# One Trainium2 core: weight decoding of the first gated layer moved into PSUM banks and off GpSimd, with later output sums and freer engine choice

## The chip, the cores and the metric

The kernel runs on one core of one Trainium2 chip. The metric is the device time of one launch in microseconds (us): lower is better. The median of three runs before the change is 941.42 us (940.76 to 943.93). PE is TensorE (matrix products), DVE is VectorE, ACT is ScalarE, POOL is GpSimd, and SP is SyncE, whose queue here issues all the transfers.

## The reference

The program computes three layers in a row, all in float32 at the interface:

```python
# 1 attention with a running state: B=4, H=8, S=768, D=48
for t in range(S):
    cur = einsum('bhd,bhe->bhde', u[None] * kt, vt)
    y[:, :, t] = einsum('bhd,bhde->bhe', rt, state + cur)
    state = wt[:, :, :, None] * state + einsum('bhd,bhe->bhde', kt, vt)
x = y.transpose(0, 2, 1, 3).reshape(3072, 384)
# 2 gated layer, d_ff = 1536
x = (1 / (1 + exp(-(x @ w_gate))) * (x @ w_val)) @ w_out
# 3 second layer, d_ff = 2048
h = x @ w_in
return (h * tanh(softplus(h))) @ w_out2
```

Matrix products of full precision are made of float16 pieces: each operand is split into a high and a low float16 part, and three products of parts are added up.

## The kernel before

The sequence is cut into 24 steps of 32 positions, j, and 12 pairs of steps, p. For a pair, POOL and DVE build the decayed inner products of the positions in `fine` (tiles blk, pt, A), DVE transposes r, k and w into RD, KD, WD and KT, PE forms the coarse scores lp, and eight small copies shared by ACT and DVE ("merges", `merge`, L664) put them into X. Then `step` runs on PE: yp (the outputs of 32 positions), xp (their transposition) and kp (the update of the state s). The copies of KT into KK ("gathers", `gather`, L705) come before kp, and yp becomes xs and then xt, the input of the gated layer for 256 rows.

The gated layer of pair p is six gates, i = 0 to 5 (`gate`). A gate has two blocks of 128 columns for the gate (weights wgs, tile gv with last digit 0) and two for the value (wvs, last digit 1). One block is nine matmuls of 128x256, called a product below. ACT takes the sigmoid, DVE multiplies (L905), ACT writes the high half of gt (L917) and DVE the rest (L920). `out1` adds the gated values times wos into three sums per pair (o10_0 is pair 0, sum 0), each in four parts of nine matmuls, in the PSUM tile of the bank po. The gates use the PSUM banks pg0 to pg3 in turn: three of them in pair 0, all four afterwards.

The weights of the gated layer arrive as float64 words. Eighteen chunks of 128x768 (six each of wg, wv, wo) are loaded into three raw tiles in turn, and each is decoded: ACT makes the low bits ("low", L239) and a rebased word (L249), DVE joins them, ACT casts the high float16 half, and a fourth instruction subtracts to get the low half (called the rest below). Before the change the even chunks (all wg) are decoded by `decode_early` in halves of 128x384, one in the PSUM bank pg3 and one in po, with the rest on DVE (L401). The odd chunks (all wv) and all of wo are decoded whole in SBUF by `decode`, with the rest on DVE or POOL (L307).

The order of the work is a plan: every `add` or `attn` call gives a task, its engine or a choice of engines with costs, and the keys it reads and writes. `Plan.run` places the tasks by due time on each engine, and the instructions are issued in that order. Engines run their own queue strictly in order and wait for each other through semaphores, so what stands behind a waiting instruction waits too.

Of the kernel before, what the change touches and what calls it, by code (L numbers as in the profile page):

```python
# [25 lines left out]
DM = H * D  # L26
# [134 lines left out]
def mixer_moe_kernel(  # L161
# [199 lines left out]
    def decode_early(name, i, dst, src, count):  # L361

        slot = count % 3
        raw = ("raw", slot)
        low = ("low", count % 2)
        key = (name, i)
        load_raw(key, lambda: dp, src, (KC, 256), slot)

        def bits3(e):
            lows[key] = dp.tile([128, KC, 256], U32, tag=f"low{count % 2}", name=f"low_{name}{i}")  # L370
            spare_bits(key)

        add("act", 1.1, bits3, [raw, "consts"], [low])
        for h in range(2):
            f = 2 * i + h
            hs = slice(128 * h, 128 * h + 128)
            fs = slice(128 * f, 128 * f + 128)
            bank = (("pg", 3), "po")[h]

            def rebase(e, h=h, hs=hs, f=f):  # L380
                pool, tag = ((pg, "pg3"), (po, "po"))[h]
                t = pool.tile([128, 512], F32, tag=tag, name=f"word_{name}{f}")
                words[name, f] = t[:, : KC * 128].rearrange("p (a b) -> p a b", a=KC)
                rebased(words[name, f], raws[key][:, :, hs, 1])

            def join(e, hs=hs, f=f):
                bits = words[name, f].bitcast(U32)
                nc.vector.scalar_tensor_tensor(
                    out=bits,
                    in0=bits,  # L390
                    scalar=3,
                    in1=lows[key][:, :, hs],
                    op0=ALU.logical_shift_left,
                    op1=ALU.bitwise_or,
                )

            def high(e, fs=fs, f=f):
                nc.scalar.copy(out=dst[:, 0, :, fs], in_=words[name, f])

            def rest(e, fs=fs, f=f):  # L400
                nc.vector.tensor_tensor(  # L401
                    out=dst[:, 1, :, fs],
                    in0=words.pop((name, f)),
                    in1=dst[:, 0, :, fs],
                    op=ALU.subtract,
                )
# [82 lines left out]
    def fine(p):  # L489
# [27 lines left out]

# [65 lines left out]
    def coarse(p, cells):  # L583
# [25 lines left out]
        def flip_w(e):  # L609

            wd[p] = w = ap.tile([128, 7, BH], F32, tag=f"WD{p % 2}", name=f"WD{p}")
            nc.vector.transpose(out=w[:, :4], in_=window(C * (DH + DP), 8 * DH, 4))
            for n, o in ((4, 4), (6, 6)):
                k = n // 2 if n == 4 else 1
                i = 0 if n == 4 else 4
                nc.vector.tensor_tensor(  # L616
                    out=w[:, o : o + k],
                    in0=w[:, i : i + 2 * k : 2],
                    in1=w[:, i + 1 : i + 2 * k : 2],
                    op=ALU.mult,  # L620
                )
# [46 lines left out]
        attn("dve", 1.05, lambda e: flip_r(e, 1), [R], [(*RD, 2)])  # L668
# [12 lines left out]
    def keys(p):  # L681
# [16 lines left out]
                in_=rows(p)[1].rearrange("p t d -> p d t"),  # L698
            )

        def gather(g, q, h):
# [3 lines left out]
            nc.scalar.copy(out=whole, in_=own)  # L705

        attn("pool", 1.0, lambda e: update(e, 8), [W], [K])
        attn("pool", 0.2, join, [], [W])
# [237 lines left out]
    def out1(p, c, part):  # L946
# [17 lines left out]

        reads = [("gt", p % 2, f // 2, a) for f in fr for a in range(2)]
        reads.append(("gt", p % 2, "tile"))
        reads += [("wo", f // 2, a) for f in fr for a in range(2)]
# [352 lines left out]
    for p in range(NP):  # L1320
        for f in range(NF1):
# [103 lines left out]
```

## Time and profile before

| what | value |
|---|---|
| median of three runs | 941.42 us |
| the profiled execution, its own time | 939.37 us |
| its span, first to last instruction | 937.7 us |
| busy: PE, DVE, ACT, POOL | 93%, 71%, 51%, 52% |
| mean granted clock of PE | 0.991 |

The shares are means over stages. In the page's forty slices (23.4 us each) PE is at 0, 4, 7, 8 and 7 tenths in the first five and at 9 from the sixth on, while DVE is at 7 to 9 and POOL at 8 to 9 tenths in the first five. All of the first layer's weights, the first three pairs of attention and the first twelve gates lie in the first 140 us.

### The profile page before, as it was taken

The page shows a single profiled execution, that of the slowest core. Times are in us where ns is not written, and L with a number is a line of the kernel's source. Part 1 is how long each engine was busy: PE and PEld are TensorE (multiplying, and loading weights), DVE is VectorE, ACT ScalarE, POOL GpSimd, SP SyncE. Part 2 cuts the span into 40 slices and gives each one's busy share as a digit, 9 for nine tenths or more (in the row PEclk, how much of TensorE's full clock was granted, in tenths as well). Part 3 has the DMA queues.
Part 4 walks back from the last instruction along what each step waited for, and adds up shares of the span by engine and source line. Part 5 has one row for each costly group of instructions (what it writes and reads, how often), then busy time and mean ns, then how long its engine had stood idle before and what let it go on. Part 6 is the DMA issues. An engine that isn't in the chain of part 4 may idle for free.

```text
span 937.7 us, 29380 instructions
## 1 busy us (share of the span) xinstructions
PE 874.2 (93%) x12808; PEld 703.9 (75%) x12808; DVE 661.3 (71%) x1094; ACT 479.1 (51%) x1065; POOL 487.7 (52%) x528
## 2 busy tenths in 40 slices
PE   0478799999999999999999999999999999999998
PEld 0366678888888888888888886667677676776788
DVE  7999985766785868677688888775655556555541
ACT  2769855352525333342528667675555655556540
POOL 8999931726565464637472275553433434334330
PEclk9989899999999999999999999999999999999999
DMA  9457742213223322232114930010200102000000
GB/s 314 135 166 227 239 119 73 60 47 81 74 60 84 83 56 72 65 85 59 53 47 119 261 102 13 12 40 2 68 1 18 52 1 69 1 19 18 1 34 35
DMA packets 56464, 71.89 MB, mean 77 GB/s; under 512 B 20752, under 2 KB 37648, under 8 KB 56208
## 3 DMA queue, kind: packets, MB, share of 16 engines
q1 hardware_dynamic: 56336, 70.03, 25.3%
q8 instruction: 100, 1.64, 0.8%
q14 instruction: 28, 0.23, 0.1%
HBM read 56.64 MB, written 9.44 MB: 70 GB/s over the span
## 4 chain that ended last, share of the span: by engine, by line
PE 78%; DVE 11%; ACT 5%; DMA 3%; issue 2%; POOL 1%; SPq 0%; ACTq 0%; DVEq 0%; POOLq 0%
PE gv L889 22%; PE h L1067 20%; PE o L1182 18%; PE o L957 13%; PE yp L737 2%; PE kp L829 2%; DVE X L664 1%; ACT X L664 1%; PE lp L643 1%; DMA raw_wp<-wo 1%; ACT KK L705 1%; DVE A L507 1%; DVE KD L605 1%; DVE WD L616 1%; DVE pt L487 1%
## 5 line engine op out<-in xcount | busy, mean ns | idle before, releaser
L1067 PE MATMUL h<-x,wis 128*128 128x512 f16 x864 | 199.9, 379 | 0.0
L889 PE MATMUL gv<-xt,wgs 128*128 128x256 f16 x1296 | 168.8, 277 | 10.5 <-DVE gt L920 7.3
L957 PE MATMUL o<-gt,wos 128*128 128x256 f16 x1296 | 166.9, 274 | 6.4 <-DVE wos L307 2.7
L889 PE MATMUL gv<-xt,wvs 128*128 128x256 f16 x1296 | 166.3, 274 | 1.3 <-DVE gt L920 0.7
L1101 POOL TENSOR_TENSOR sum<-e 128x256 f32<-128x256 f32 x96 | 71.4, 744 | 183.1 <-ACT e L1078 182.9
L487 POOL TENSOR_TENSOR blk<-blk 128x384 f32<-128x384 f32 (+3 forms) x139 | 123.6, 904 | 53.2 <-DMA blk<-rkw 33.7
L889 PEld LDWEIGHTS <-wgs 128*128 128x128 f16 x1296 | 126.5, 99 | 28.9 <-ACT X L664 6.0
L1067 PEld LDWEIGHTS <-wis 128*128 128x128 f16 x864 | 83.5, 98 | 82.9
L957 PEld LDWEIGHTS <-wos 128*128 128x128 f16 x1296 | 125.7, 98 | 25.8 <-DVE wos L307 3.4
L889 PEld LDWEIGHTS <-wvs 128*128 128x128 f16 x1296 | 126.4, 98 | 18.0 <-POOL wvs L307 1.1
L487 POOL TENSOR_TENSOR pt<-blk 128x384 f32<-128x384 f32 x93 | 107.0, 1175 | 50.3 <-DMA blk<-rkw 48.8
L1078 ACT ACTIVATE e<-h 128x512 f32<-128x512 f32 x96 | 57.3, 597 | 84.1 <-PE h L1067 83.2
L900 ACT ACTIVATE sig<-gv 128x512 f32<-128x512 f32 x72 | 43.0, 600 | 86.3 <-PE gv L889 86.0
L917 ACT CAST gt<-gv 128x512 f16<-128x512 f32 x72 | 42.0, 584 | 72.8 <-DVE gv L905 72.6
L1182 PE MATMUL o<-wps,gt 128*128 128x192 f16 x612 | 74.0, 246 | 0.0
L905 DVE SCALAR_TENSOR_TENSOR gv<-gv,sig 128x512 f32<-128x512 f32 x72 | 50.4, 702 | 25.6 <-PE gv L889 20.3
L624 POOL TENSOR_TENSOR RD<-RD,WD 128x256 f32<-128x256 f32 (+2 forms) x32 | 33.6, 1050 | 63.2 <-PE lp L643 32.9
L1120 DVE SCALAR_TENSOR_TENSOR gt<-e,gt 128x256 f16<-128x256 f32 x41 | 27.5, 682 | 49.7 <-ACT gt L1115 49.7
L920 DVE TENSOR_TENSOR gt<-gv,gt 128x512 f16<-128x512 f32 x72 | 49.3, 684 | 16.6 <-ACT gt L917 15.6
L1182 PE MATMUL o<-wps,wgs 128*128 128x192 f16 x498 | 59.4, 246 | 0.0
L664 ACT COPY X<-lp 24x64 f32<-24x64 f32 x159 | 40.7, 256 | 34.1 <-DVE X L664 25.9
L1182 PE MATMUL o<-wps,wos 128*128 128x192 f16 x456 | 57.1, 246 | 0.0
(109 smaller groups left out, 1490.4 us busy)
## 6 DMA issues: line engine op xcount, KB each, us to landing
v<-vt SPq DMA_DIRECT2D x96, 96.0 KB, 2.6
blk<-rkw SPq DMA_DIRECT2D x22, 384.0 KB, 3.8
raw_wi<-wi SPq DMA_DIRECT2D x8, 768.0 KB, 5.1
raw_wp<-wo SPq DMA_DIRECT2D x8, 768.0 KB, 5.8
blk<-rkw SPq DMA_DIRECT2D x11, 512.0 KB, 3.9
raw_wg<-wg SPq DMA_DIRECT2D x6, 768.0 KB, 6.2
raw_wv<-wv SPq DMA_DIRECT2D x6, 768.0 KB, 6.5
raw_wo<-wo SPq DMA_DIRECT2D x6, 768.0 KB, 5.4
```

Of the source, the lines that this page charges most:

```text
L487: engines[e].tensor_tensor(out=pv, in0=a, in1=b, op=ALU.mult)
L664: put(out=xp[p][o : o + t, xs, t:], in_=lps[p, e][i : i + t, :, c : c + C - t])
L889: nc.tensor.matmul(gps[p, i, o][:, h], w[:, a, kc, fs], xt[p][:, c, kc, :], start=(n == 0), stop=(n == 3 * KC - 1),)
L900: nc.scalar.activation(out=sgs[p, i], in_=gps[p, i, 0], func=AF.Sigmoid, scale=1.0 / (SW * SX))
L905: nc.vector.scalar_tensor_tensor(out=gps[p, i, 1], in0=gps[p, i, 1], scalar=SG / (SW * SX), in1=sgs.pop((p, i)), op0=ALU.mult, op1=ALU.mult,)
L917: nc.scalar.copy(out=gt[p][:, 0, 2 * i : 2 * i + 2], in_=gps[p, i, 1])
L920: nc.vector.tensor_tensor(out=gt[p][:, 1, 2 * i : 2 * i + 2], in0=gps[p, i, 1], in1=gt[p][:, 0, 2 * i : 2 * i + 2], op=ALU.subtract,)
L957: nc.tensor.matmul(ops[p, c][:, :NT], wos[:, a, f, cs], gt[p][:, g, f, :], start=(f == 0 and n == 0), stop=(f == NF1 - 1 and n == 2),)
L1067: nc.tensor.matmul(hps[r, f], w2["wi"][:, a, kc, fs], x2[r][:, c, kc, :], start=(n == 0), stop=(n == 3 * KC - 1),)
L1078: nc.scalar.activation(out=es[r, f], in_=hps[r, f], func=AF.Mish, scale=ih)
L1101: engines[e].tensor_tensor(out=sums[0][:, n - 1], in0=a(), in1=b(), op=op)
L1182: nc.tensor.matmul(ops2[h, first], home(slots[r, i, name])[:, c, tsl], w2["wp"][:, a, w, i, :], start=(new and n == 0), stop=(n == 3 * NF2 ...
```

## The change

Four edits, all of them in how the first 140 us are planned, though the last reaches all pairs.

- All eighteen chunks go through `decode_early`: halves of 128x384, the even block in bank pg3, the odd one in po, the rest always on DVE. POOL has no decoding left in this layer. A half of wo is one block f, so wos is now written block by block.
- The gates keep to three banks until gate 8 (6p+i up to `FREE`), because pg3 is in use for longer.
- The parts of pair 0's output sums are issued by the table `FIRST`, from f = 2 of pair 1 on, where one part per f stood before.
- The planner may put gathers on ACT or DVE, the product with U on DVE or POOL, and the two joining products of WD on DVE or POOL.

```diff
-WHOLE = range(1, 12, 2)
+FIRST = ((), (), (0,), (1,), (2,), (3,), (4,), (5,), (6, 7), (8,), (9,), (10, 11))
+FREE = 8
...
-            bank = (("pg", 3), "po")[h]
...
+            w = [(name, i if name == "wo" else f, a) for a in range(2)]
+            w = [(*x, h) if name == "wo" else x for x in w]
             add("act", 0.43, rebase, [raw, "table1"], [bank])
             add("dve", 0.48, join, [low], [bank])
-            add("act", 0.39, high, [bank], [(name, f, 0)])
-            add("dve", 0.47, rest, [bank, (name, f, 0)], [(name, f, 1)])
+            add("act", 0.39, high, [bank], [w[0]])
+            add("dve", 0.47, rest, [bank, w[0]], [w[1]])
...
-                attn("dve", 1.2, times_u, ["U"], [pt])
+                attn({"dve": 1.2, "pool": 1.9}, 0, times_u, ["U"], [pt])
...
-        attn("dve", 1.3, flip_w, [W], [WD])
+        attn("dve", 0.32, flip_w, [W], [WD])
+        attn({"dve": 1.3, "pool": 0.7}, 0, joined_w, [], [WD])
...
-                        "act", 0.51, lambda e, a=(g, q, h): gather(*a), ["KT"], [("KK", p % 2, g, q, h)]
+                        {"act": 0.51, "dve": 0.47},
...
-        n = 4 if p else 3
+        n = 4 if 6 * p + i > FREE else 3
...
-            if p > 0:
+            if p == 1:
+                for n in FIRST[f]:
+                    out1(0, n // 4, n % 4)
+            elif p:
...
-            if count in WHOLE:
-                load_raw((name, i), lambda: dp, in_cols(w, cs), (KC, 256), count % 3)
-                part = lambda dst=dst, cs=cs: dst[:, :, :, cs]
-                both = [2 * i, 2 * i + 1]
-                decode((name, i), part, (KC, 256), count, count % 3, (), W1HI, W1LO, False, both)
-            else:
-                decode_early(name, i, dst, in_cols(w, cs), count)
+            decode_early(name, i, dst, in_cols(w, cs), (KC, 256), count, halves)
...
-        decode(("wo", i), dst, (2, DM), i, i % 3, (), W1HI, W1LO)
+        decode_early("wo", i, wos, in_rows(wo1, cs), (2, DM), count, halves)
```

Where the planner moves the queues shows at three places.

POOL, before pair 0's first scores. lp0 on PE waits for the first two products of RD0 with WD0. Before:

```order
L487 TENSOR_TENSOR pt_161<-blk1_135 128x768
L624 TENSOR_TENSOR RD0_158<-RD0_158,WD0_165 128x32x8
L487 TENSOR_TENSOR pt_175<-blk1_135 128x384
L624 TENSOR_TENSOR RD0_158<-RD0_158,WD0_165 128x32x16
L487 TENSOR_TENSOR blk1_135<-blk1_135 128x16x24
```

and after:

```order
L486 TENSOR_TENSOR pt_148<-blk1_119 128x768
L486 TENSOR_TENSOR pt_154<-blk1_119 128x384
L486 TENSOR_TENSOR blk0_95<-blk0_95 128x4x24
L486 TENSOR_TENSOR blk1_119<-blk1_119 128x16x24 x2
L486 TENSOR_TENSOR blk0_95<-blk0_95 128x2x8x24
L486 TENSOR_TENSOR pt_181<-blk1_119 128x8x48 x2
L626 TENSOR_TENSOR RD0_156<-RD0_156,WD0_175 128x32x8
L486 TENSOR_TENSOR blk0_95<-blk0_95 128x24
L626 TENSOR_TENSOR RD0_156<-RD0_156,WD0_175 128x32x16
```

Work on blk1 (pair 1) that followed RD0 now precedes it.

DVE, around gate 0 of pair 0, whose last instruction (gt0) frees the bank for the third gate. KT is pair 1's transposed k, X1 its merged scores. Before:

```order
L696 STREAM_TRANSPOSE KT_92<-blk1_135 128x24x32
L905 SCALAR_TENSOR_TENSOR gv0_0_1_605<-gv0_0_1_605,sig_645 128x512
L401 TENSOR_TENSOR wgs_88<-word_wg4_529,wgs_88 128x3x128
L388 SCALAR_TENSOR_TENSOR word_wg5_571<-word_wg5_571,low_wg2_517 128x384
L487 TENSOR_TENSOR pt_569<-pt_569,U_94 128x768
L507 TENSOR_REDUCE A_91<-pt_592 128x16
L507 TENSOR_REDUCE A_91<-pt_569 128x32
L507 TENSOR_REDUCE A_91<-pt_663 128x8x2x2
L920 TENSOR_TENSOR gt0_784<-gv0_0_1_605,gt0_784 128x512
L624 TENSOR_TENSOR RD1_509<-RD1_509,WD1_576 128x32x24
L664 COPY X1_620<-lp1_0_717 24x8x8
```

and after, in two pieces, the first up to the first merge, the second from the last merge on:

```order
L913 SCALAR_TENSOR_TENSOR gv0_0_1_605<-gv0_0_1_605,sig_647 128x512
L389 SCALAR_TENSOR_TENSOR word_wg4_588<-word_wg4_588,low_wg2_518 128x384
L389 SCALAR_TENSOR_TENSOR word_wg5_617<-word_wg5_617,low_wg2_518 128x384
L699 STREAM_TRANSPOSE KT_92<-blk1_119 128x24x32
L402 TENSOR_TENSOR wgs_88<-word_wg4_588,wgs_88 128x3x128
L709 COPY KK_93<-KT_92 32x16x24 x4
L666 COPY X1_651<-lp1_0_718 24x8x8
```

```order
L666 COPY X1_651<-lp1_1_719 24x8x8
L666 COPY X1_651<-lp1_1_719 16x8x16
L666 COPY X1_651<-lp1_1_719 8x8x24
L928 TENSOR_TENSOR gt0_680<-gv0_0_1_605,gt0_680 128x512
L389 SCALAR_TENSOR_TENSOR word_wv4_887<-word_wv4_887,low_wv2_595 128x384
```

Four gathers have come to DVE, the product with U and three sums have left this place, and gt0 has moved from before the merges to behind them.

DVE after the change, before the first output sum o10_0, which takes the bank po once the last odd half (word_wo11) is done. X2 and KT are pair 2's:

```order
L666 COPY X2_1582<-lp2_0_1512 8x8x24
L389 SCALAR_TENSOR_TENSOR word_wo9_1616<-word_wo9_1616,low_wo4_1497 128x384
L848 TENSOR_TENSOR s4_904<-kp3_1_1181,s4_904 128x384
L699 STREAM_TRANSPOSE KT_92<-blk2_279 128x24x32
L402 TENSOR_TENSOR wos_90<-word_wo9_1616,wos_90 128x384
L913 SCALAR_TENSOR_TENSOR gv1_0_1_1397<-gv1_0_1_1397,sig_1414 128x512
L709 COPY KK_93<-KT_92 32x16x24
L389 SCALAR_TENSOR_TENSOR word_wo11_1715<-word_wo11_1715,low_wo5_1584 128x384
L709 COPY KK_93<-KT_92 32x16x24 x2
L402 TENSOR_TENSOR wos_90<-word_wo11_1715,wos_90 128x384
```

Before the change the wo chunks stood ahead of KT and of X2's merges, and o10_0's first two parts ahead of all of pair 1's gates on PE; now two and a half gates, lp2 and yp4 stand ahead of o10_0.

## Rows read from the trace of the kernel before

**Rows 1.** Stretches: length, busy PE, PEld, DVE, ACT, POOL, granted clock, DMA share, GB/s

```profile
66.00:97.00 31.00, 26.68 (x541) 20.58 (x539) 28.65 (x51) 26.98 (x54) 30.36 (x27) 0.89 0.63 205
97.00:105.00 8.00, 3.17 (x16) 1.76 (x17) 8.00 (x8) 7.24 (x10) 7.84 (x7) 0.69 0.64 204
...
140.00:500.00 360.00, 355.90 (x6870) 314.28 (x6868) 263.01 (x420) 141.00 (x337) 192.06 (x200) 1.00 0.25 66
```

**Rows 2.** Timeline of PE: start, us, instruction, count, idle before

```profile
23.48 1.78 PE L643 MATMUL lp<-RD,KD 64*32 64x48 f32 x128 [23.48 <-POOL blk L487]
...
48.99 2.10 PE L889 MATMUL gv<-xt,wgs 128*128 128x256 f16 x9
...
65.79 2.08 PE L889 MATMUL gv<-xt,wgs 128*128 128x256 f16 x9 [5.90 <-DVE gt L920]
...
76.63 3.53 PE L889 MATMUL gv<-xt,wgs 128*128 128x256 f16 x18
...
96.72 0.27 PE L957 MATMUL o<-gt,wos 128*128 128x256 f16 x1
...
99.81 0.28 PE L957 MATMUL o<-gt,wos 128*128 128x256 f16 x1 [1.94 <-ACT wos L304]
102.61 1.46 PE L957 MATMUL o<-gt,wos 128*128 128x256 f16 x6 [2.52 <-DVE wos L307]
...
105.33 1.88 PE L889 MATMUL gv<-xt,wgs 128*128 128x256 f16 x9
...
133.00 1.16 PE L889 MATMUL gv<-xt,wvs 128*128 128x256 f16 x9
133.99 1.15 PE L957 MATMUL o<-gt,wos 128*128 128x256 f16 x9
```

**Rows 3.** Timeline of POOL, the work on blk1

```profile
22.40 2.03 POOL L487 TENSOR_TENSOR blk<-blk 128x384 f32<-128x384 f32 x2
```

**Rows 4.** DVE, 10 to 125 us by shape: count, busy us, mean ns, idle before

```profile
L293 DVE SCALAR_TENSOR_TENSOR word_wo<-word_wo,low_wo 128x768 uint32<-128x768 uint32 x6 | 8.4, 1421 | 0.0
...
L293 DVE SCALAR_TENSOR_TENSOR word_wv<-word_wv,low_wv 128x768 uint32<-128x768 uint32 x6 | 7.3, 1219 | 0.1
L388 DVE SCALAR_TENSOR_TENSOR word_wg<-word_wg,low_wg 128x384 uint32<-128x384 uint32 x12 | 6.6, 551 | 0.3 <-ACT word_wg L249 0.3
L401 DVE TENSOR_TENSOR wgs<-word_wg,wgs 128x384 f16<-128x384 f32 x12 | 6.5, 544 | 0.0
...
L487 DVE TENSOR_TENSOR pt<-pt,U 128x768 f32<-128x768 f32 x3 | 4.1, 1377 | 0.0
...
L307 DVE TENSOR_TENSOR wos<-word_wo,wos 128x768 f16<-128x768 f32 x2 | 3.4, 1751 | 0.0
```

**Rows 5.** POOL, the same stretch by shape

```profile
L307 POOL TENSOR_TENSOR wvs<-word_wv,wvs 128x768 f16<-128x768 f32 x5 | 8.6, 1720 | 0.4 <-ACT wvs L304 0.3
L307 POOL TENSOR_TENSOR wos<-word_wo,wos 128x768 f16<-128x768 f32 x4 | 6.6, 1655 | 0.4 <-ACT wos L304 0.3
```

**Rows 6.** ACT, the same stretch by shape

```profile
L705 ACT COPY KK<-KT 32x384 f32<-32x384 f32 x24 | 12.2, 508 | 0.5 <-DVE KT L696 0.2
L249 ACT ACTIVATE word_wg<-raw_wg 128x384 f32<-128x384 f32 x12 | 6.1, 519 | 0.0
L239 ACT ACTIVATE low_wg<-raw_wg,floor 128x768 uint32<-128x768 uint16 x6 | 6.1, 1014 | 10.4 <-DMA raw_wg<-wg 10.3
```

**Rows 7.** Timeline of ACT, pair 1's merges, first and last

```profile
65.39 1.68 ACT L664 COPY X<-lp 24x64 f32<-24x64 f32 x6
...
70.91 0.83 ACT L664 COPY X<-lp 24x64 f32<-24x64 f32 x3 [0.98 <-DVE X L664]
```

**Rows 8.** Timeline of DVE, copies within SBUF beside an idle and a busy POOL

```profile
530.07 0.36 DVE L347 CAST wps<-word_wp 128x384 f16<-128x384 f32 x1 [1.68 <-DMA xt<-xs]
...
550.27 0.92 DVE L347 CAST wps<-word_wp 128x192 f16<-128x192 f32 x1
```

**Rows 9.** DMA issues: count, KB each, median us to landing

```profile
raw_wv<-wv SPq DMA_DIRECT2D x6, 768.0 KB, 6.5
```

More of the change, by code (lines that the diff above doesn't have):

```diff
@@ L359, in combine, with decode_early @@
             add(cost, 0, lambda e, n=n: rest(e, n), [src, (*key, 0, n)], [(*key, 1, n)])
-    def decode_early(name, i, dst, src, count):
+    def decode_early(name, i, dst, src, n, count, halves):
         slot = count % 3
@@ L366, in decode_early, with rebase, join @@
         key = (name, i)
-        load_raw(key, lambda: dp, src, (KC, 256), slot)
+        load_raw(key, lambda: dp, src, n, slot)
         def bits3(e):
-            lows[key] = dp.tile([128, KC, 256], U32, tag=f"low{count % 2}", name=f"low_{name}{i}")
+            lows[key] = dp.tile([128, *n], U32, tag=f"low{count % 2}", name=f"low_{name}{i}")
             spare_bits(key)
-        add("act", 1.1, bits3, [raw, "consts"], [low])
-        for h in range(2):
+        add("act", 1.0, bits3, [raw, "consts"], [low])
+        for h, (part, put) in enumerate(halves):
             f = 2 * i + h
-            hs = slice(128 * h, 128 * h + 128)
-            fs = slice(128 * f, 128 * f + 128)
             bank = (("pg", 3), "po")[h]
-            def rebase(e, h=h, hs=hs, f=f):
+            def rebase(e, h=h, part=part, f=f):
                 pool, tag = ((pg, "pg3"), (po, "po"))[h]
                 t = pool.tile([128, 512], F32, tag=tag, name=f"word_{name}{f}")
-                words[name, f] = t[:, : KC * 128].rearrange("p (a b) -> p a b", a=KC)
-                rebased(words[name, f], raws[key][:, :, hs, 1])
-            def join(e, hs=hs, f=f):
+                shape = raws[key][:, :, :, 1][part]
+                t = t[:, : KC * 128].rearrange("p (a b) -> p a b", a=shape.shape[1])
+                words[name, f] = t
+                rebased(t, shape)
+            def join(e, part=part, f=f):
                 bits = words[name, f].bitcast(U32)
@@ L395, in join, with high, rest @@
                 )
[L397 to L400 removed]
+            def high(e, put=put, f=f):
+                nc.scalar.copy(out=dst[put(0)], in_=words[name, f])
+            def rest(e, put=put, f=f):
                 nc.vector.tensor_tensor(
[L402 removed]
+                    out=dst[put(1)],
                     in0=words.pop((name, f)),
[L404 removed]
+                    in1=dst[put(0)],
                     op=ALU.subtract,
                 )
+            w = [(name, i if name == "wo" else f, a) for a in range(2)]
+            w = [(*x, h) if name == "wo" else x for x in w]
             add("act", 0.43, rebase, [raw, "table1"], [bank])
             add("dve", 0.48, join, [low], [bank])
[L410 to L411 removed]
+            add("act", 0.39, high, [bank], [w[0]])
+            add("dve", 0.47, rest, [bank, w[0]], [w[1]])
     blk = {}
@@ L615, in flip_w @@
                 i = 0 if n == 4 else 4
-                nc.vector.tensor_tensor(
+                engines[e].tensor_tensor(
                     out=w[:, o : o + k],
@@ L699, in flip, with gather @@
             )
-        def gather(g, q, h):
+        def gather(on, g, q, h):
             o, n = 64 * g + 32 * q, 64 * g + 32 * h
@@ L704, in gather @@
             whole = KK[o : o + 32, p % 2, :, h, :DH].rearrange("p (e i) d -> p e i d", e=2)
-            nc.scalar.copy(out=whole, in_=own)
+            put = nc.scalar.copy if on == "act" else nc.vector.tensor_copy
+            put(out=whole, in_=own)
         attn("pool", 1.0, lambda e: update(e, 8), [W], [K])
@@ L714, in keys @@
                     attn(
-                        "act", 0.51, lambda e, a=(g, q, h): gather(*a), ["KT"], [("KK", p % 2, g, q, h)]
+                        {"act": 0.51, "dve": 0.47},
+                        0,
+                        lambda on, a=(g, q, h): gather(on, *a),
+                        ["KT"],
+                        [("KK", p % 2, g, q, h)],
                     )
@@ L966, in out1 @@
         reads.append(("gt", p % 2, "tile"))
-        reads += [("wo", f // 2, a) for f in fr for a in range(2)]
+        reads += [("wo", f // 2, a, f % 2) for f in fr for a in range(2)]
         if bank == "po2":
@@ L1270, in mixer_moe_kernel @@
     for i in range(6):
-        cs = slice(256 * i, 256 * i + 256)
         for name, dst, w in (("wg", wgs, wg), ("wv", wvs, wv)):
-            if count in WHOLE:
-                load_raw((name, i), lambda: dp, in_cols(w, cs), (KC, 256), count % 3)
-                part = lambda dst=dst, cs=cs: dst[:, :, :, cs]
-                both = [2 * i, 2 * i + 1]
-                decode((name, i), part, (KC, 256), count, count % 3, (), W1HI, W1LO, False, both)
-            else:
-                decode_early(name, i, dst, in_cols(w, cs), count)
+            cs = slice(256 * i, 256 * i + 256)
+            halves = []
+            for f in range(2 * i, 2 * i + 2):
+                h = 128 * (f % 2)
+                fs = slice(128 * f, 128 * f + 128)
+                part = (slice(None), slice(None), slice(h, h + 128))
+                halves.append((part, lambda a, fs=fs: (slice(None), a, slice(None), fs)))
+            decode_early(name, i, dst, in_cols(w, cs), (KC, 256), count, halves)
             count += 1
@@ L1282, in mixer_moe_kernel @@
         cs = slice(2 * i, 2 * i + 2)
-        dst = lambda cs=cs: wos[:, :, cs]
-        load_raw(("wo", i), lambda: dp, in_rows(wo1, cs), (2, DM), i % 3)
-        decode(("wo", i), dst, (2, DM), i, i % 3, (), W1HI, W1LO)
+        halves = []
+        for f in range(2 * i, 2 * i + 2):
+            part = (slice(None), slice(f % 2, f % 2 + 1))
+            halves.append((part, lambda a, f=f: (slice(None), a, slice(f, f + 1))))
+        decode_early("wo", i, wos, in_rows(wo1, cs), (2, DM), count, halves)
+        count += 1
     def tail1(p):
```

6 lines of the change are left out of this document (4 added, 2 removed).

## Prediction

> **What bounds the kernel now.** I read the stretches first: from 140 us on PE is busy for 355.9 of 360 us at full granted clock, so whatever the change does there is hidden behind PE [rows 1]. Ahead of that it is the other way round: from 66 to 97 us DVE is busy for 28.65 of 31 us, ACT 26.98 and POOL 30.36, with PE at a clock of 0.89, and from 97 to 105 DVE has no gap at all while PE works for 3.17 of 8 us at 0.69 [rows 1]. The kernel's time is therefore the PE work, which stays the same, plus what PE loses before some 133 us. The timeline of PE shows where: 23.48 us until the first scores, a first gate product only at 48.99, 5.90 us ahead of the third gate, which waits for its bank, and from 96.72 to 105.33 the first output sum, which waits for one wos chunk after another [rows 2]. Two products of nine matmuls start 0.99 us apart when nothing is missing [rows 2]; that is the unit below.
>
> **What the change takes off and puts on each engine.** POOL loses five rests of 1.72 and four of 1.66 us, 15.2 us [rows 5], and gains three products with U. DVE gains those nine chunks: halves in PSUM last 0.55 us but are queued back to back, so the record overlaps; two halves of rest cost about 0.94 us a chunk [rows 4], 8.5 us in all. It saves on the joins: whole ones took 1.22 to 1.42 us [rows 4], two halves 0.94, so 12 x 0.38 = 4.5. Its own three whole rests (1.75) become 0.94: 2.4 less [rows 4]. Three products with U of 1.38 us may leave, 4.1 [rows 4], but twelve gathers of pairs 0 to 2 come. A gather is a copy of fp32 within SBUF; on DVE the trace has such a copy of 384 columns at 0.36 us beside an idle POOL and one of half the size at 0.92 beside a busy one [rows 8]. That is 4.3 to 11 us for twelve. DVE's sum is 8.5 - 4.5 - 2.4 - 4.1 + 4.3 to 11, or +1.8 to +8.5, less the joins of WD that may move to POOL, which no row shows and which I bound by one product with U for each pair, 0 to 4: about no relief for the engine that is already full. ACT loses twelve gathers of 0.508, 6.1 us [rows 6], and casts and rebases as much as before.
>
> **Where PE feels it, in order of time.** (1) On POOL five more instructions on pair 1's blk1 stand ahead of RD0; one costs about 1.0 us, two 2.03 [rows 3]. lp0 moves from 23.48 to about 26.4. Behind it DVE's transposition of A bounds the merges of X0, so that I let only 0.8 us of the 2.9 through. The eight gathers that follow, 8 x 0.508 = 4.1 us on ACT [rows 6], are split between two engines: 2.1 less. The first gate product moves from 48.99 to 47.7, -1.3.
>
> (2) X1's merges begin earlier, at about 62.6 instead of 65.39, and take as long as before, 6.35 us from the first to the last on two engines [rows 7]. But gate 0's last instruction now stands behind all of them on DVE, and the third gate needs its bank: it begins at about 69.0 + 0.6 = 69.6 instead of 65.79. With yp2 already done by then, the fourth gate starts at about 76.1 instead of 76.63 [rows 2]. PE is 0.5 ahead, and 0.8 of the first gain is given back.
>
> (3) From there to 97 us the three engines that decode stay full, as the sums above say. Output sums no longer come, so PE does two products of pair 1 by the time at which o10_0 began: 2.0 us ahead.
>
> (4) Between 96.72 and the end of yp5 at 133.00 PE runs 21 products before the change, 20.7 us, and some 5.4 us of lp, yp and kp; 36.3 - 26.1 = 10.2 us are lost to waits (1.94 and 2.52 the largest) and slow clock [rows 2]. That loss goes, and three waits come in its place, each read off the new order. Two gates of pair 1 are wanted before the last weights and banks are free: 1.4 us behind the transposition of KD. lp2's merges, X2, now stand late, with yp4 right behind two and a half gates: 4.2 us. And o10_0 takes bank po only after the last half of wo (word_wo11), which stands on DVE behind X2, KT of pair 2 and three gathers: about 118 us by the durations, 5.0 us after PE is ready. With 2 us of slow clock behind such waits (PE's clock was 0.69 over the stall of before [rows 1]) that is 12.6. So 12.6 - 10.2 = +2.4 against the lead of 2.0: **+0.4**.
>
> (5) Two costs on top. Of the gathers' range I counted the low end, since POOL has 15 us less to do; POOL was 98% busy, so some copies must meet one. The price is 0 to +4.5 (eight gathers of pairs 1 and 2 by 0.92 - 0.36 = 0.56); I take +0.5, nearer to 0 because four of the twelve, pair 0's, stand beside as many on ACT. And the new halves release a raw tile only after the second rebased word, 0.52 us later than a whole one would [rows 6], as I read the two forms, in twelve chunks over three tiles in turn: 12 x 0.52 / 3 = 2.1 at most. ACT waited 10.3 us for such transfers before, and each takes 6.5 us [rows 6, 9], so the price is 0 to +2.1; I take +0.5, as ACT has six us more room. (The cost could be below nothing if POOL's shorter queue also released blk earlier; that is in the faster rival.)
>
> **The sum:** +0.4 + 0.5 + 0.5 = +1.4 on the profiled execution's 939.37, 940.8. The median of the runs lies 2.05 above that execution, so **942.8**. A measurement of this kernel can tell about 0.3%, 2.8 us, from no change: this is no change.
>
> [...] Whole joins with two operands in SBUF took 1.22 us in the mean for wv and 1.42 for wo, the same shape, while halves with one operand in PSUM took 0.55, less than half of either [rows 4]. [...]
>
> **Rivals.**
> - Slower, 946.3: the gathers decide. Each of the eight in pairs 1 and 2 waits for a POOL instruction, 8 x 0.56 = 4.5, and with the +0.4 that gives 939.37 + 4.9 + 2.05. For it: POOL 98% and DVE 92% busy from 66 to 97 [rows 1], the 0.92 row [rows 8]. Against: POOL loses 15 us. It decides from a mean above some 0.7 us for a gather on DVE.
> - Faster, 936.0: the three new waits are half as long (5.3 for 10.6) and bring half of the slow clock, because joins that meet no POOL let DVE run ahead of the sum of durations. 0.4 - 5.3 - 1.0 = -5.9, with half of (5) -5.4, and 939.37 - 5.4 + 2.05 = 936.0. For it: all of POOL's decoding, 15.2 us, is gone at the place where all four are full. Against: DVE's sum is no smaller, and it is DVE that has no gap from 97 to 105.
> - That the change does not do what it says: POOL's order has no decoding left, so only the free choices could fall back; under 0.02.
>
> **How the numbers follow.** Forecast, no measurable change: 0.40, its own range 939 to 944.2 (to the measurable bound). Slower rival: 0.30, with the ring's 2.1 too 948.4. Faster rival: 0.30, and 930.7 if none of the new waits appears. To hold 0.8, the range goes from 935 to 948: both rivals' centres lie inside, a third of each outside. Faster by over 0.3% 0.30, within 0.3% 0.40, slower by over 0.3% 0.30.
>
> **What would show it.** Step (1) is right if the first gate product starts near 47.7, and wrong if lp0's delay shows there in full (51). Step (2): PE idle until about 69.6 before the third gate, released by gate 0's rest. Step (4): PE waits of about 4 us for X2 and 5 us for wos between 105 and 118, and a clock below 1 behind them; if they are short, the faster rival holds. Step (5): a mean of gathers on DVE near 0.4 or 0.9, and ACT's idle time on raw transfers. The whole is wrong if PE still has gaps of over 2 us after 140, since then the early ledger does not set the time.

## The result and the profile after

The kernel became slower: 954.69 us (952.09 to 955.5, six runs) against 942.12, a ratio of 1.0129, 95% interval 1.0114 to 1.0144. The forecast was 942.8 with a range up to 948, so the measured time lies outside it. The profiled execution has 954.49 us and a span of 952.6, 14.9 more than before. Below, the cost of a run is its ratio, less one, times 942: the change costs 12.2 us (10.7 to 13.6).

The stretches after the change, in the columns of [rows 1]:

```profile
66.00:97.00 31.00, 20.22 (x486) 15.70 (x486) 26.25 (x54) 21.64 (x52) 12.74 (x16) 0.78 0.50 160
97.00:105.00 8.00, 5.47 (x46) 4.08 (x46) 7.98 (x16) 7.25 (x14) 5.42 (x4) 1.00 0.87 268
140.00:500.00 360.00, 356.33 (x6925) 314.24 (x6924) 270.47 (x426) 126.87 (x313) 196.59 (x217) 1.00 0.28 75
```

From 140 us on PE is as full as before, so the loss was made ahead of that. From 66 to 97 us PE works 6.5 us less, and POOL only 12.74 of 31 us instead of 30.36: the work was taken off POOL, and nothing on PE came earlier for it. The timeline of PE has the marks of [rows 2]:

```profile
28.34 1.79 PE L645 MATMUL lp<-RD,KD 64*32 64x48 f32 x128 [28.34 <-POOL RD L626]
...
52.70 2.08 PE L897 MATMUL gv<-xt,wgs 128*128 128x256 f16 x9 [1.25 <-ACT xt L773]
...
69.27 0.36 PE L745 MATMUL yp<-v,X 64*32 64x48 f32 x2 [4.58 <-ACT X L666]
...
72.21 0.36 PE L745 MATMUL yp<-v,X 64*32 64x48 f32 x2 [2.58 <-DVE X L666]
...
77.57 4.00 PE L897 MATMUL gv<-xt,wgs 128*128 128x256 f16 x18 [1.77 <-DVE gt L928]
...
85.24 2.16 PE L897 MATMUL gv<-xt,wgs 128*128 128x256 f16 x18
...
124.55 0.45 PE L745 MATMUL yp<-v,X 64*32 64x48 f32 x10 [4.40 <-ACT wos L399]
...
129.88 2.08 PE L965 MATMUL o<-gt,wos 128*128 128x256 f16 x9 [3.46 <-DVE wos L402]
```

The first scores come 4.9 us later than in [rows 2], the first gate product 3.7, the third gate 11.8 (with yp2 done before it now) and the fourth gate 8.6, so more than half of the loss is there by 85 us. What DVE did ahead of the third gate shows in its timeline, with the four gathers of pair 0, the four of pair 1 and then three of pair 2:

```profile
36.46 3.92 DVE L709 COPY KK<-KT 32x384 f32<-32x384 f32 x4
...
64.17 2.09 DVE L699 STREAM_TRANSPOSE KT<-blk 128x768 f32<-128x768 f32 x1
66.03 0.62 DVE L402 TENSOR_TENSOR wgs<-word_wg,wgs 128x384 f16<-128x384 f32 x1
66.66 4.55 DVE L709 COPY KK<-KT 32x384 f32<-32x384 f32 x4
71.24 0.92 DVE L666 COPY X<-lp 24x64 f32<-24x64 f32 x3
...
76.83 0.69 DVE L928 TENSOR_TENSOR gt<-gv,gt 128x512 f16<-128x512 f32 x1
...
127.37 0.33 DVE L709 COPY KK<-KT 32x384 f32<-32x384 f32 x1
127.70 0.57 DVE L389 SCALAR_TENSOR_TENSOR word_wo<-word_wo,low_wo 128x384 uint32<-128x384 uint32 x1
128.30 0.71 DVE L709 COPY KK<-KT 32x384 f32<-32x384 f32 x2
```

A gather took 0.98 and 1.14 us in the first two pairs and 0.33 to 0.36 in the third. POOL's timeline tells the difference: at 66 us it goes from one long product to the next (busy 3.92 of 4 us from 66 to 70), and around 127 us it is idle (0 of 5 us from 126 to 131). At 36 us, beside pair 0's gathers, it is as busy (all 4 us from 36 to 40).

```profile
35.41 4.10 POOL L486 TENSOR_TENSOR pt<-blk 128x384 f32<-128x384 f32 x4
...
64.22 1.99 POOL L486 TENSOR_TENSOR blk<-blk 128x384 f32<-128x384 f32 x2
66.30 2.06 POOL L486 TENSOR_TENSOR pt<-blk 128x384 f32<-128x384 f32 x2
68.32 1.59 POOL L626 TENSOR_TENSOR RD<-RD,WD 128x768 f32<-128x768 f32 x1
69.88 2.18 POOL L486 TENSOR_TENSOR pt<-blk 128x384 f32<-128x384 f32 x2
...
134.46 1.62 POOL L817 TENSOR_TENSOR s<-s,WD 128x384 f32<-128x384 f32 x2 [9.10 <-DVE s L848]
```

All eight of pairs 0 and 1 stand ahead of what PE wants: pair 0's ahead of xs, pair 1's ahead of the merges of X1, which PE meets with the waits of 4.58 and 2.58 us above.

### The profile page after: what moved, and what is told of

Read it like the earlier page. It is cut to its first block, busy times and chain, and to the rows that moved or that the text cites. A ratio compares the mean times of both kernels' runs of the same rounds, so it can differ in the third digit from the quotient of the medians.

```text
span 952.6 us, 29437 instructions
## 1 busy us (share of the span) xinstructions
PE 875.6 (92%) x12808; PEld 704.8 (74%) x12808; DVE 669.6 (70%) x1138; ACT 463.4 (49%) x1055; POOL 474.4 (50%) x542
## 4 chain that ended last, share of the span: by engine, by line
PE 78%; DVE 11%; ACT 3%; DMA 3%; issue 2%; POOL 2%; SPq 0%; DVEq 0%; ACTq 0%; POOLq 0%
PE gv L897 22%; PE h L1075 20%; PE o L1190 17%; PE o L965 13%; PE kp L837 2%; PE yp L745 2%; PE lp L645 1%; DMA raw_wg<-wg 1%; ACT X L666 1%; DVE X L666 1%; DVE KK L709 1%; DVE KD L604 1%; DVE A L506 1%; DVE word_wp L294 1%; POOL sum_wp L334 1%
## 5 line engine op out<-in xcount | busy, mean ns | idle before, releaser
L965 PEld LDWEIGHTS <-wos 128*128 128x128 f16 x1296 | 126.3, 98 | 24.7 <-issue 6.1
L486 POOL TENSOR_TENSOR blk<-blk 128x384 f32<-128x384 f32 (+2 forms) x138 | 116.1, 857 | 35.7 <-DMA blk<-rkw 23.7
L666 ACT COPY X<-lp 24x64 f32<-24x64 f32 x168 | 42.9, 255 | 34.9 <-DVE X L666 25.5
L1190 PEld LDWEIGHTS <-gt 128*128 128x128 f16 x612 | 52.9, 98 | 3.3
```

The costliest lines, as they stand in the source:

```text
L486: engines[e].tensor_tensor(out=pv, in0=a, in1=b, op=ALU.mult)
L666: put(out=xp[p][o : o + t, xs, t:], in_=lps[p, e][i : i + t, :, c : c + C - t])
L965: nc.tensor.matmul(ops[p, c][:, :NT], wos[:, a, f, cs], gt[p][:, g, f, :], start=(f == 0 and n == 0), stop=(f == NF1 - 1 and n == 2),)
L1190: nc.tensor.matmul(ops2[h, first], home(slots[r, i, name])[:, c, tsl], w2["wp"][:, a, w, i, :], start=(new and n == 0), stop=(n == 3 * NF2 ...
```

## The experiments

Theory A is the gathers on DVE, theory B the opening (lp0 late), theory C the decoding in halves, theory D the sensitivity of the plan, theory E (in e10 to e12) the wo chunks that hold bank po ahead of the first sum. Each run was timed beside the kernel before on the same chip.

| run | ratio to before | 95% interval | cost, us | lp0, us | lp3, us |
|---|---|---|---|---|---|
| before | 1 | | 0 | 23.48 | 160.81 |
| the change | 1.0129 | 1.0114 to 1.0144 | 12.2 | 28.34 | 173.36 |
| e1 gathers on ACT | 1.0076 | 1.0050 to 1.0102 | 7.2 | 28.49 | 171.31 |
| e2 before, gathers free | 1.0100 | 1.0070 to 1.0130 | 9.4 | 23.44 | 168.73 |
| e3 no free choice | 1.0075 | 1.0049 to 1.0102 | 7.1 | 29.63 | 170.85 |
| e4 old sums | 1.0080 | 1.0052 to 1.0107 | 7.5 | 28.42 | 170.05 |
| e5 e1 and old sums | 1.0059 | 1.0028 to 1.0089 | 5.6 | 28.49 | 166.41 |
| e6 decoding alone | 1.0072 | 1.0047 to 1.0096 | 6.8 | 27.24 | 168.15 |
| e7 before, late sums | 1.0002 | 0.9985 to 1.0018 | 0.2 | 23.40 | 163.59 |
| e8 e5, old rule for RD | 1.0036 | 1.0022 to 1.0050 | 3.4 | 25.36 | 165.27 |
| e9 before, one cost | 1.0035 | 1.0021 to 1.0050 | 3.3 | 25.07 | 166.48 |
| e10 wv in halves | 1.0097 | 1.0075 to 1.0118 | 9.1 | 27.11 | 172.49 |
| e11 wo in halves | 0.9995 | 0.9977 to 1.0013 | -0.5 | 23.43 | 163.16 |
| e12 e6, old cost | 1.0039 | 1.0021 to 1.0056 | 3.7 | 27.12 | 164.90 |
| e13 e12, lp0 first | 1.0057 | 1.0039 to 1.0075 | 5.4 | 26.48 | 167.57 |
| e14 e1, lp0 first | 1.0108 | 1.0080 to 1.0135 | 10.2 | 27.61 | 170.02 |
| e15 price 1.05 | 1.0089 | 1.0066 to 1.0112 | 8.4 | 28.41 | 172.67 |
| e16 wo halves, late sums | 1.0016 | 1.0005 to 1.0028 | 1.5 | 23.38 | 166.43 |
| e17 e12, old opening | 1.0092 | 1.0073 to 1.0111 | 8.7 | 24.66 | 171.21 |
| e18 e1, old opening | 1.0029 | 1.0014 to 1.0044 | 2.7 | 24.76 | 167.19 |

The last two columns are the starts of the scores of pairs 0 and 3 on PE, the second by when PE waits little more.

**e1, gathers on ACT in the change.**

```diff
-                        {"act": 0.51, "dve": 0.47},
+                        {"act": 0.51},
```

> The changed kernel with all gathers of KT into KK on ACT again, everything else as changed. Theory A (gathers on DVE beside a busy POOL last about 1 us, 3.92 us for four in pair 0 and 4.55 in pair 1, and stand ahead of what PE waits for): the time falls by 5 to 9 us, to some 946 to 950 us, and the third gate starts about 5 us earlier than 77.57. Theory B (the loss is POOL's order ahead of pair 0's first scores, lp0 4.9 us later): the time stays within 2 us of 954.7. Theory C (the decoding through two PSUM banks and the late output sums cost it): also within 2 us, with the waits of about 4.4 us for X2 and 3.5 us for wos still there.

The cost fell from 12.2 to 7.2 us, and the third gate came 10 us earlier:

```profile
67.16 3.55 PE L897 MATMUL gv<-xt,wgs 128*128 128x256 f16 x18 [4.00 <-DVE gt L928]
...
121.13 0.44 PE L837 MATMUL kp<-v,KK 32*64 32x48 f32 x2 [4.98 <-ACT KK L709]
123.78 0.45 PE L837 MATMUL kp<-v,KK 32*64 32x48 f32 x4 [2.21 <-ACT KK L709]
125.34 1.94 PE L837 MATMUL kp<-v,KK 32*64 32x48 f32 x58 [1.10 <-ACT KK L709]
127.20 2.10 PE L965 MATMUL o<-gt,wos 128*128 128x256 f16 x9
```

The ten us are not the gathers' length alone: in e1 the planner also puts gate 0's rest back ahead of X1's merges on DVE (66.32 and 68.91 us). At the fourth gate, where the same PE work lies behind both, e1 is 6.9 us ahead (78.36 against 85.24), and at lp3 only 2.1. What lies between shows in the lines of kp: pair 2's gathers, which the change had in part on DVE beside an idle POOL, now stand late on ACT, and kp waits 8.3 us for them. The products that PE has done in gates and sums by a given time say the same; they are counted from its records:

| by | before | the change | e1 |
|---|---|---|---|
| 97 us | 24 | 18 | 22 |
| 105 us | 26 | 23 | 29 |
| 135 us | 47 | 36 | 38 |

By 105 us e1 is ahead of the kernel before, and what it still costs shows on PE between 105 and 135 us.

**e2, the free choice in the kernel before.** The same two-engine cost put into the kernel before, and nothing else.

```diff
-                        "act", 0.51, lambda e, a=(g, q, h): gather(*a), ["KT"], [("KK", p % 2, g, q, h)]
+                        {"act": 0.51, "dve": 0.47},
+                        0,
+                        lambda on, a=(g, q, h): gather(on, *a),
```

> The kernel before with only the gathers' engine left free (ACT or DVE at the same two costs as in the change). Theory A: 4 to 9 us slower than before, 946 to 951 us, with DVE gathers of about 1 us in pairs 0 to 2. Theories B and C: within 2 us of before's 942.

9.4 us slower with lp0 where it was. Its gathers, by shape, from 10 to 125 us, on either engine (seven of the sixteen of pairs 0 and 1 are on DVE):

```profile
L706 DVE COPY KK<-KT 32x384 f32<-32x384 f32 x7 | 6.7, 960 | 0.1
...
L706 ACT COPY KK<-KT 32x384 f32<-32x384 f32 x9 | 4.6, 508 | 0.4 <-DVE KT L696 0.3
```

In its timeline of DVE the four of pair 1 take 4.28 us, and in that of PE the third gate waits for the rest of wgs that stands behind them:

```profile
62.93 4.28 DVE L706 COPY KK<-KT 32x384 f32<-32x384 f32 x4
```

```profile
67.84 0.82 PE L894 MATMUL gv<-xt,wgs 128*128 128x256 f16 x3 [3.77 <-DVE wgs L401]
```

e1 and e2 together show theory A from both sides: the free choice of engine costs. They show less of its size, since either edit moves other work too: in e2 the wait in view is 3.8 of the 9.4 us. They also show that it is not all.

**e3, no free choice.** Gathers on ACT, the product with U and the joins of WD on DVE again.

```diff
-                attn({"dve": 1.2, "pool": 1.9}, 0, times_u, ["U"], [pt])
+                attn({"dve": 1.2}, 0, times_u, ["U"], [pt])
-        attn({"dve": 1.3, "pool": 0.7}, 0, joined_w, [], [WD])
+        attn({"dve": 1.0}, 0, joined_w, [], [WD])
```

> The changed kernel with gathers on ACT, the product with U on DVE and the joins of WD on DVE: only the decoding and the output sums differ from before. If the free choices are the whole cost, it comes to 942 within 3 us; if the decoding and the sums cost something themselves (theory C), it stays 5 us or more above before; if theory B holds it depends on lp0: POOL's order has the same work on blk1 ahead of RD0, so lp0 stays near 28 and the time near 947.

7.1 against e1's 7.2: the other two choices are worth nothing here, and decoding and sums with the opening cost 7 us without any choice.

**e4, the old sums in the change; e5, with gathers on ACT too.**

```diff
-            if p == 1:
-                for n in FIRST[f]:
-                    out1(0, n // 4, n % 4)
-            elif p:
+            if p > 0:
```

> The changed kernel with pair 0's output sums in the old places, one part for each f of pair 1. Theory C: the sums in the old place meet the decoded wos even later, so the time is 0 to 6 us longer; if the new table is itself the loss, the time falls by 3 us or more. Theories A and B: within 2 us of 954.7, since all of their loss lies before the first sum.

> The changed kernel with gathers on ACT and pair 0's output sums in the old places. If the two losses found so far (5.5 and 4.7 us) are separate, they add: about 944.5 us, within 2 us of before. If both are the same stall seen twice, it stays near 949.

In e4 the time fell by 4.7 us, which is the second branch of theory C (the new table is itself a loss) and against A and B as they were put. With gathers on ACT the same edit is worth 1.6 (7.2 to 5.6), within the intervals nothing, so the two losses do not simply add. Read the other way, gathers on ACT are worth 5.0 us with the new table (e1) and 1.9 with the old one (7.5 to 5.6), where the intervals overlap.

**e6, the decoding alone.** As e5, with U and WD on DVE and the old rule for RD (e8): only decoding, banks and one cost of the plan differ from before.

> The kernel before with the decoding alone changed: all eighteen chunks in halves in the two PSUM banks, the rests on DVE, three gate banks until gate 8; gathers, product with U, joins of WD, their order rule and the sums as before. Theory C (the decoding itself costs, through the two banks that both chunks and gates or sums want, and through DVE): 947 us or more. Theories A and B: 942 within 3 us; if PSUM joins that meet no POOL help DVE, it is faster than before, 937 to 940.

6.8 us slower. POOL is idle for more than half of the stretch in which it was full, DVE and ACT are nearly as full as before:

```profile
66.00:97.00 31.00, 24.34 (x507) 18.72 (x508) 27.73 (x57) 26.53 (x62) 13.53 (x15) 0.81 0.56 185
```

**e7, late sums in the kernel before.** The table FIRST and its use, nothing else.

> The kernel before with only the table of later output sums. If the stall at 97 to 105 us is paid once and its work is then hidden elsewhere, the time falls by 3 to 6 us, to 937 to 940. If PE then meets the merges of X2 and the later sums instead, as the profile of the change suggests (waits of 4.4 and 3.5 us there), it is within 2 us of before or up to 4 us slower.

No change. The stall at 97 to 105 us goes and another comes: PE waits for the gathers of pair 2, behind work on ACT.

```profile
118.40 0.44 PE L830 MATMUL kp<-v,KK 32*64 32x48 f32 x2 [4.18 <-ACT KK L706]
120.49 0.45 PE L830 MATMUL kp<-v,KK 32*64 32x48 f32 x4 [1.65 <-ACT KK L706]
```

**e8, the rule for RD.** The change also holds a rule that RD's second part is transposed after its first. It is not in the cut diff above, and no step of the prediction counts it.

```diff
-        attn("dve", 1.05, lambda e: flip_r(e, 1), [R, (*RD, 0)], [(*RD, 2)])
+        attn("dve", 1.05, lambda e: flip_r(e, 1), [R], [(*RD, 2)])
```

> As the run with gathers on ACT and the old sums, and without the new rule that RD's second part is transposed after its first (a dependency in the plan). Theory B: lp0 comes back from 28.4 to 24 to 26 us and the time falls by 2 to 4 us against that run. Theory A alone: lp0 moves but the time stays within 1.5 us, since DVE's transposition of A and the merges end no earlier.

lp0 came 3.1 us earlier than in e5, and the cost went from 5.6 to 3.4; the intervals overlap.

**e9, one cost of the plan.** The decoding's low bits are entered at 1.0 instead of 1.1 in the change. In the kernel before:

```diff
-        add("act", 1.1, bits3, [raw, "consts"], [low])
+        add("act", 1.0, bits3, [raw, "consts"], [low])
```

> The kernel before with one number changed: the plan's cost of the low bits of the wg chunks, 1.1 to 1.0, as in the change. The first product of RD0 on POOL stays first and another goes to DVE, so the queues shift. Theory D (any shift of the plan near the start moves the time by several us): 2 to 5 us off before's 942. Theory C (the decoding costs by what it does): within 1.5 us of before.

3.3 us slower with the same instructions: theory D. A single number that moves the order is worth as much as an edit, and no difference of 3 us between two of these plans can be put down to an edit by itself.

**e10, e11, e12: only wv, only wo, all chunks in halves, at the old cost.** e10 and e11 leave the other chunks of wv and wo decoded whole, as before. They differ in one thing more: e10 has four gate banks from pair 1 on, as before, and e11 and e12 have three until gate 8.

> The kernel before with only the six wv chunks decoded in halves in the two banks (wo whole in SBUF with the rest on DVE or POOL, costs of the plan as before). Theory C: both banks are taken in turn by four steps that alternate between ACT and DVE, so twelve gate chunks cost at one place what POOL took beside: 3 to 5 us slower than before, with PE waiting for wvs or wgs. Theory E (it is the wo chunks holding bank po ahead of the first sum): within 1.5 us of before.

> The kernel before with only the six wo chunks decoded in halves in the two banks, and three gate banks until gate 8. Theory E: the first sum waits for bank po until the last half of wo is done, 3 to 6 us slower than before with a wait of PE for wos of 3 us or more. Theory C: 2 to 3 us slower. If the work taken off POOL helps there: 0 to 3 us faster than before.

> All eighteen chunks in halves as in the run of the decoding alone, but with the plan's old cost of 1.1 for the low bits. Theories C and E: 946 to 950, like that run. Theory D: anything from 941 to 952.

wv in halves costs 9.1 us, wo in halves nothing. All chunks in halves cost 3.7, less than wv alone: theory E fell, and theory C holds for wv in sign, not in size. Why all in halves cost less than wv alone is not shown: the bank rule for gates 6 to 8 differs between e10 and e12, and so does the order of the plan. From 66 to 97 us, first e10 and then e11:

```profile
66.00:97.00 31.00, 21.86 (x495) 16.73 (x495) 28.03 (x58) 24.80 (x57) 15.33 (x17) 0.78 0.66 206
```

```profile
66.00:97.00 31.00, 20.67 (x472) 15.98 (x473) 26.13 (x53) 23.17 (x48) 26.90 (x26) 0.69 0.65 197
```

PE is less busy in e11, at no cost, than in e10, at 9.1 us, and 6 us less than before: how full PE is from 66 to 97 us does not by itself set the time.

**e13 and e14, lp0 first.** Dependencies put RD0, WD0 and KD0 ahead, and the updates of pair 1 behind lp0:

```diff
+            first = [("lp", 0)] if p == 1 else []
-            attn(one, 0, lambda e, f=update: f(e, 0), [W], [R])
+            attn(one, 0, lambda e, f=update: f(e, 0), [W, *first], [R])
```

> All eighteen chunks in halves with the old cost, as in e12, and pair 0's transpositions and products for lp0 put ahead of the work on pair 1 by dependencies in the plan. Theory B: lp0 is back at 24 to 25 us and the time falls from 946.5 to 941 to 944. Theory C: lp0 is back, and the time stays within 1.5 us of 946.5.

> The changed kernel with gathers on ACT, as in e1, and the same order ahead of lp0 as in e13; the new table of sums stays. Theory B: from 949.2 to 944 to 946. Theory C: within 1.5 us of 949.

They did not do what they were made for: halves of wg and wv slipped in between the transpositions, lp0 came only 0.6 and 0.9 us earlier, and the first gate product later than in e12 and e1. Nothing follows on B or C; e14 also ended 3.0 us above e1, with overlapping intervals.

**e15, the true price.**

```diff
-                        {"act": 0.51, "dve": 0.47},
+                        {"act": 0.51, "dve": 1.05},
```

> The changed kernel with the plan's price of a gather on DVE set to 1.05 us, near what the trace shows beside a busy POOL, instead of 0.47. The choice stays free, and the plan still gives DVE as many groups of gathers. If the price was the mistake: 948 to 951, near the run with gathers on ACT. If the choice itself is: above 952, since the plan still fills DVE where it thinks it idle.

8.4 us (6.2 to 10.6 by its interval): less than the change, not told from e1. The planner now puts 27 gathers on DVE where the change had 40, and of pairs 0 and 1 six where it had eight (what the expectation calls groups are rows of the timeline, not copies). Only one of the six stands between KT of pair 1 and X1's merges, and together they take 3.87 us instead of 8.47:

```profile
36.53 2.17 DVE L709 COPY KK<-KT 32x384 f32<-32x384 f32 x2
...
39.38 0.39 DVE L709 COPY KK<-KT 32x384 f32<-32x384 f32 x1
...
64.85 0.59 DVE L709 COPY KK<-KT 32x384 f32<-32x384 f32 x1
...
72.67 0.72 DVE L709 COPY KK<-KT 32x384 f32<-32x384 f32 x2
```

So this run, too, goes the way of theory A.

**e16, the two harmless parts together:** e7's table in e11.

> The kernel before with wo in halves (e11) and the later sums (e7), which alone changed nothing. If the sums are then no longer in front of the decoding of wo and POOL is free of wo: 937 to 940. If the time lost is only moved on: within 2.5 us of before.

1.5 us slower than before, so no part of the change was found that beats the kernel before; its stall at 97 us was paid elsewhere again.

**e17 and e18, the opening of before.** The first halves' joins and pair 1's product with U are held behind pair 0's transpositions, the updates of pair 1 behind lp0, and the rule for RD (e8) is as before. The cut shows the first of these:

```diff
+    marks["r0", 0].deps.add(marks["w", 0])
+    marks["kd", 0].deps.update((marks["r0", 0], marks["w", 0]))
+    marks["x", 0].deps.add(marks["kd", 0])
+    joins[0].deps.add(marks["kd", 0])
+    for t in joins[1:]:
+        t.deps.add(marks["x", 0])
```

> All eighteen chunks in halves (e12), with the opening of before: the joins of the first halves held until KD0 and X0's transposition are issued, pair 1's product with U and updates behind lp0. lp0 should start at 23 to 24.5 us and the first gate product near 49. Theory B: 941 to 944, within 2 us of before. Theory C: 945 to 948, like e12, with the loss seen between the first gate product and the third step's scores.

> The changed kernel with gathers on ACT, the joins of WD on DVE and the opening of before as in e17; product with U still free, table of later sums as changed. Theory B: from 949.2 (e1) to 943 to 946. Theory C: 947 or more.

lp0 is back at 24.7 us in both. e18 gained 4.5 us on e1, as theory B said (the joins of WD, which it also takes back, are worth nothing by e3). But its first gate product comes only 0.5 us earlier than e1's (50.83 against 51.35), so the gain is made behind the opening. e17 lost 5.0 on e12, which B excludes. A part of the early start is given back in e17 at the third gate, behind the merges of X1:

```profile
69.42 4.00 PE L907 MATMUL gv<-xt,wgs 128*128 128x256 f16 x18 [6.78 <-ACT X L673]
```

So the opening is not a fixed price on every plan. Holding it to the old order was worth 4.5 us in the change without its gathers, and how it reaches the end is not shown.

## Why the prediction was wrong

What held: PE is the bound after 140 us (busy for 356.33 of 360) and the whole change acts ahead of that; the transfers into the raw tiles matter little. ACT waited 3.9 us for them from 20 to 130 us, 3.1 before; the 10.3 us that the prediction names is one wait, for the first chunk, which ends at 12.41 us. The new waits for X2 and for the first sum are there with about their size, 4.40 and 3.46 us against 4.2 and 5.0, but some ten us later than the forecast. Not all of the 4.40 is X2's: the line names a cast of ACT, and in the timeline of DVE the last merge that yp4 needs there ends at 123.28, 1.3 us before yp4 starts:

```profile
122.32 0.96 DVE L666 COPY X<-lp 24x64 f32<-24x64 f32 x3 [0.90 <-ACT X L666]
```

**The step whose failure is best shown is (5), the gathers' price.** The sum took the lower end, 0.36 us each, "since POOL has 15 us less to do", and 0.5 us on top. The eight of pairs 0 and 1 took 3.92 + 4.55 = 8.47 us; at 0.36 they would be 2.9. That is 5.6 us more; with 0.5 us forecast, taking them off DVE gave back 5.0 (e1, with the order that goes with it). POOL's relief over 100 us did not help these eight, which met POOL at work: at the two places where they stand, after KT of pairs 0 and 1, POOL was busy for 4 of 4 us (36 to 40) and 3.92 of 4 (66 to 70). The slower rival had the mechanism and the point from which it decides (a mean above 0.7; it was 1.06 for these eight, 0.82 for the twelve of pairs 0 to 2). That it nearly had the price (4.5) is luck in part: it charged pairs 1 and 2, and the dear ones were pairs 0 and 1. It was given 0.30, though for a stretch where POOL is 98% busy [rows 1] the row of 0.92 beside a busy POOL [rows 8] was the nearer one. And its 946.3 is still 8.4 us short: with all gathers on ACT 7.2 us remain (e1), so other steps failed too.

The trace of the change has the mechanism in its records: each of the eight gathers beside a POOL at work ended 0.21 to 0.22 us after the end of a POOL instruction. The longest, 1.55 us from 68.59 on, ended at 70.14; the product of RD on POOL, 1.59 us from 68.32 on, had ended at 69.92. The eight took 0.98 and 1.14 us in the mean of their pairs, the other 32, all beside an idle POOL, 0.33 to 0.36, and the halves with an operand in PSUM 0.53 to 0.62 (0.54 to 0.58 for the 38 beside a busy one, 0.53 to 0.62 for the 27 beside an idle one). Why a POOL instruction holds up the copy was not shown.

**Step (1) failed too.** It saw five more instructions on POOL, lp0 at 26.4, and let 0.8 us of the delay through. lp0 started at 28.34. One reason is the rule for RD: it moves the joins of WD on DVE, POOL waits for them, and without it lp0 comes 3.1 us earlier (e5 to e8). It is not the only one, since lp0 is at 27.2 in e6 and 27.1 in e12, which have the old rule. In the timelines of DVE, before and after, and of POOL, after, the joins end at 20.5 and at 23.7 us, and POOL has stood idle for 1.87 us:

```profile
20.00 0.52 DVE L616 TENSOR_TENSOR WD<-WD 128x32 f32<-128x32 f32 x1
```

```profile
23.29 0.42 DVE L618 TENSOR_TENSOR WD<-WD 128x64 f32<-128x64 f32 x2
```

```profile
23.57 1.00 POOL L486 TENSOR_TENSOR blk<-blk 128x384 f32<-128x384 f32 x1 [1.87 <-DVE WD L618]
```

Then the gathers on DVE held xs, instead of saving 2.1 us: the first gate product came at 52.70, where 47.7 was forecast. In e18, without the gathers and with lp0 at 24.76, it is at 50.83. I had read POOL's order at this place and DVE's not.

**Step (2)** forecast the third gate at 69.6 and the fourth at 76.1; they came at 77.57 and 85.24. The order it named is right (merges first, then gate 0's rest at 76.83). The 8 us are the late start and, by e1, the gathers with the order that goes with them: X1's last merge on DVE ends at 76.81, where 69.0 was forecast.

**Step (3)** took it that the three engines that decode stay full and go on at their old pace. From 66 to 97 us POOL worked 12.74 of 31 us, ACT 21.64 (26.98 before) and DVE 26.25 (28.65). The last rest of wv ended at 104.9 us (95.4 before) and that of wo at 138.5 (115.3 before, and 130.0 in e7, at no cost). What a slower decoding costs by itself is not settled. Ten plans have all chunks in halves and gathers on ACT (e1, e3, e5, e6, e8, e12, e13, e14, e17, e18), and they cost 2.7 to 10.2 us. In e6, e10, e12, e17 and e18 POOL is busy for only 7.7 to 19.8 of 31 us, while DVE and ACT, which take all four steps of a half between them, stay at 27.7 to 28.4 and 24.8 to 27.1; but in e8, which costs 3.4, POOL is at 27.9. In e6 the joins of a wg half and a wv half come in pairs that start 3.0 and 3.7 us apart, in the timeline of DVE:

```profile
90.12 0.57 DVE L389 SCALAR_TENSOR_TENSOR word_wv<-word_wv,low_wv 128x384 uint32<-128x384 uint32 x1 [0.26 <-ACT word_wv L250]
90.60 0.56 DVE L389 SCALAR_TENSOR_TENSOR word_wg<-word_wg,low_wg 128x384 uint32<-128x384 uint32 x1
...
93.13 0.57 DVE L389 SCALAR_TENSOR_TENSOR word_wg<-word_wg,low_wg 128x384 uint32<-128x384 uint32 x1
93.61 0.56 DVE L389 SCALAR_TENSOR_TENSOR word_wv<-word_wv,low_wv 128x384 uint32<-128x384 uint32 x1
...
96.80 0.57 DVE L389 SCALAR_TENSOR_TENSOR word_wv<-word_wv,low_wv 128x384 uint32<-128x384 uint32 x1 [0.26 <-ACT word_wv L250]
```

That fits a loop through two banks that ACT and DVE take in turn, but a run with a third bank for it was not made, the one run that points at wv alone (e10) is one plan, and e9 shows that 3 us come and go with the order alone.

**Step (4)** was right in kind, gaining the stall and paying it back, and e7 shows the same in the kernel before, at no gain. It was too small: from 97 to 135 us PE did about 18 products where it did 23 before, some 4.5 us lost against 2.4 forecast, and the first sum came at 129.88 us, not at some 118. In e1, which is ahead at 105 us, the first sum came no earlier than 127.20, so by this count it is here, and not from 66 to 97 us, that PE pays for what remains in e1.

Taken away in one order, the 12.2 us are 5.0 for the gathers (e1), 4.5 for the opening once the gathers are gone (e18 against e1), and 2.7 that remain. In another order they are other numbers: the gathers are worth 1.9 with the old sums (e4 to e5), and the opening loses 5.0 in e17. So that gathers on DVE beside a busy POOL cost time is shown (e1, e2, e15, and the lengths of the copies); the cause of the other 7 us, opening, decoding or the order that the planner happens to find, stays open.

## What to carry to other kernels

Price a copy that moves to another engine by what the trace shows at the place where it will stand, not by a mean: here the same shape on DVE took 0.33 to 0.36 us beside an idle POOL and 0.65 to 1.55 beside a busy one. Taking work off an engine helps only if something that PE waits for comes earlier by it; here POOL's busy time from 66 to 97 us fell from 30.36 to 12.74 us and PE's with it, from 26.68 to 20.22. A lead at one mark is not a gain at the end: e1's 6.9 us at the fourth gate were 2.1 at lp3. When a planner sets the order, compare the queues of every engine at the first point where the order differs, and change one number that should not matter to learn how large the noise of the plan is, before a gain of that size is believed.

## What the runs showed of the hardware that was not expected

The same copy of 32x384 within SBUF on DVE took 0.328 to 1.547 us in the profiled execution of the change: the eight beside a busy POOL 0.65 to 1.55 us each, 1.06 in the mean, the 32 beside an idle one 0.33 to 0.36. On ACT its 56 copies took 0.507 to 0.513. So for this shape, in this execution, ACT was the steady engine, and DVE was faster in all 32 copies beside an idle POOL and slower in all eight beside a busy one.
